# 64-bit weights converted in tiles of 512 columns, two in flight, instead of 256 columns, three in flight

## The chip, the core and the metric

The kernel runs on one core of a Trainium2 chip. The core has a matrix engine (TensorE, PE in the profile), an element-wise engine (VectorE, DVE), an activation engine (ScalarE, ACT), a general engine (GpSimd, POOL) and a queue from which this kernel issues all its DMAs (SyncE, SP). Each engine takes its own instructions in the order in which they were written into its queue, and waits at an instruction until what it needs is there. The metric is the device time of one execution, in microseconds (us).

## The reference, cut to what matters

Three stages follow each other on a batch of 8 sequences of 576 tokens and width 512.

1. Attention with 8 heads: a pack of 32 rows attends to the keys and values, and then the queries attend to the result. The output is `x`.
2. A channel mix: `xk` and `xr` are blends of `x` and of `x` one token earlier; `k = relu(xk @ w_k)`, `v = (k*k) @ w_v`, `r = sigmoid(xr @ w_r)`; the output is `r * v`.
3. A second mix: `u = x + (x^T U V)^T` along the tokens, then `u + relu(u @ w_ch1) @ w_ch2`.

The activations q, k, v, p come as 32-bit floats. The weights `w_k`, `w_v`, `w_r`, `U`, `V`, `w_ch1` and `w_ch2` come as **64-bit** floats, which no engine reads. So the kernel loads them as pairs of 32-bit words and rebuilds 32-bit floats from the bits: the high word holds sign, exponent and 20 bits of fraction, the low word the rest. That is the conversion which the change touches.

## The kernel before, in words

Matmuls with the weights run in three passes of a rounded format: each operand is split into a high part and a low remainder (`split`, line 868: one copy on ACT or DVE, one subtraction on DVE), and `PASS` multiplies high by high, high by low and low by high.

The batch is treated in 4 pairs of sequences. Attention is done in 16 units (4 for each pair). The first four units run interleaved at the start; the later ones run beside the channel mix of the pair before. The channel mix and the second mix go through 12 chunks of 384 tokens. For each chunk of the channel mix, `r_block` makes three outputs from `w_r`, `k_block(m)` eight from `w_k`, and `v_block(m)` adds eight contributions of `w_v`. The second mix comes after, chunk by chunk, and is made of matmuls that hold PE to the end.

**The order of the work** is not written by hand. Every operation is recorded in a `Plan`, and `emit` (line 333) makes a list schedule: at each step it takes the engine that can start first by its own cost table, and on this engine the ready operation with the lowest class (`cls`), and within a class the one that was ready first (PE and SP: the one recorded first). The result is a fixed order for each engine. Attention has class 0. The mixes have class 1. Conversions of `w_r` and of the first half of `w_k` have class 0, those of `w_v`, of the second half of `w_k` and of `U` class 1, those of `V`, `w_ch1` and `w_ch2` class 3.

**A conversion** (`Cast.run`, line 829) takes a tile of at most N = 256 columns. It loads it into `st`, 256 pairs of words, and then runs: ACT `a` = absolute value of the high words (line 853), DVE `h` = the high words, with values under a threshold set to nought (line 854), ACT `m` = the low words as a float, scaled (line 855), then DVE in turn: shift `h` into `a` (line 857), merge bits into `a` (858), keep sign and exponent in `h` (859), `m*h` (860), `m+a` (861), and last the split into the weight's two halves, or a store to DRAM. The high words lie 8 bytes apart in `st`; `h`, `a` and `m` are tiles of their own without gaps. There are 3 buffers of `st` and 3 of each of `h`, `a`, `m`. A buffer of `st` is free for the next load as soon as `a`, `h` and `m` have read it.

`cast_rows` (line 887) converts a weight tile of 128 rows by 512 columns in two such halves; a matmul waits for the column half that it reads. `w_r` is 4 tiles of 512 columns, `w_k` and `w_v` are 8 each, `w_ch1` and `w_ch2` 16 each. The loads of the first attention units are mixed with those of `w_r` (`FIRST`, line 502), and the loads that come after a `w_r` tile wait until that tile has its `st` buffer (`go`, line 902). The second half of `w_k` and `w_v` are converted in the order v0, v1, first column halves of `w_k`, v2, v3, second column halves of `w_k`, v4 to v7. From chunk 1 on, 9 conversions for the second mix are recorded in each chunk (`NPER`, line 1202); their results go to DRAM (`w1_d`, `w2_d`) and come back later.

Of the kernel before, what the change touches and what calls it, by code (L numbers as in the profile page):

```python
# [9 lines left out]
F32 = mybir.dt.float32  # L10
F32R = mybir.dt.float32r
I32 = mybir.dt.int32
# [457 lines left out]
def packed_attention_moe_mixer_kernel(  # L470
# [19 lines left out]
    NP = p.shape[2]  # L490
    P = 128
    DM = H * D
    NJ = DM // P
    NBP = B // 2
    NI = S // 64
    NC = NI // 3
    CW = 3 * P
    MK = w_k.shape[1] // P
# [9 lines left out]
    plan = Plan(nc)  # L508
    add, sub, mul = ALU.add, ALU.subtract, ALU.mult

    def open_pool(es, name, bufs, side):
        return es.enter_context(tc.tile_pool(name=name, bufs=bufs, side=side, reuse_waits="tile"))
# [8 lines left out]
    def dtile(name, shape, parts=(0,)):  # L521
        return plan.fixed(dram.tile(shape, F32, name=name), parts)
# [4 lines left out]
    v_d = dtile("v_d", [NP, S])  # L527
    w1_d = [dtile(f"w1_d{m}", [P, NJ * P]) for m in range(MC)]
    w2_d = [dtile(f"w2_d{m}", [P, DM]) for m in range(MC)]
# [289 lines left out]


    class Cast:
        N = 256

        def __init__(self, es, side):
            self.st = Pool(obj=open_pool(es, "cvst", 3, side), bufs=3)
            self.tp = Pool(obj=open_pool(es, "cvtp", 3, side), bufs=3)
            self.pools = [self.st, self.tp]

        def run(self, srcs, n, put=None, parts=None, after=()):
            N = self.N  # L830
            raw = srcs[0][1].dtype != F32
            st = plan.tile(self.st, [P, N * 2], I32, "st", parts=tuple(range(len(srcs))))
            for i, (rows, src) in enumerate(srcs):
                s = st.at(i)
                to = s[rows, 0:2 * n] if raw else s[rows, 0:n].bitcast(F32)
                if raw:
                    src = src.bitcast(I32)
                if src.shape[0] > P:
                    to = to.rearrange("p (a c) -> p a c", a=2)
                    src = src.rearrange("(a p) c -> p a c", p=P)  # L840
                plan.dma(to, src, after=after)
            if not raw:
                if parts is None:
                    put(st.bitcast(F32))
                else:
                    split(*parts, st.bitcast(F32)[:, 0:n])
                return st.alloc
            r = slice(srcs[0][0].start, srcs[-1][0].stop)
            sv = st.rearrange("p (n t) -> p n t", t=2)[r, 0:n]
            whole = [plan.tile(self.tp, [P, N], F32, tag) for tag in "ham"]  # L850
            h, a, m = [t[r, 0:n] for t in whole]
            top = sv[:, :, 1].bitcast(F32)
            plan.act(a, top, AF.Abs)
            plan.stt(h, a, 1.125 * 2.0 ** -15, top, ALU.is_ge, mul)
            plan.act(m, sv[:, :, 0].bitcast(U32), AF.Copy, scale=2.0 ** -52)
            hb, ab = h.bitcast(I32), a.bitcast(I32)
            plan.ts(ab, hb, 3, 0x3FFFFFF8, ALU.logical_shift_left, ALU.bitwise_and)
            plan.stt(ab, hb, -0x40000000, ab, ALU.bitwise_and, ALU.bitwise_or)
            plan.ts(hb, ab, -0x800000, None, ALU.bitwise_and)
            plan.tt(m, m, h, mul)  # L860
            plan.tt(m, m, a, add)
            if parts is None:
                put(whole[2])
            else:
                split(*parts, m)
            return st.alloc

    def split(hi, lo, src, engs=("dve",)):
        plan.copy(hi, src, ("act", "dve"))
        plan.tt(lo, src, hi, sub, engs)  # L870
# [6 lines left out]
    def wtile(pl, name):  # L877
        return plan.tile(pl, [P, 2, 512], F32R, name, parts=(0, 1))

    cast_cls = [0]  # L880
    cv = Cast(es_att, "right")
# [2 lines left out]
    A0 = Bufs(es_att, "A", "right", 8)  # L884
    AX_ = [A0] + [Bufs(es_st, n, "left", 4, True) for n in "BCD"]

    def cast_rows(t, src, halves=(0, 1)):
        for h in halves:
            plan.cls = cast_cls[0]
            to = [t.at(h)[:, i, h * 256:(h + 1) * 256] for i in range(2)]  # L890
            last = cv.run([(slice(0, P), src[:, h * 256:(h + 1) * 256])], 256, parts=to)
            plan.cls = 0
        return last

    wr = [wtile(w1a, f"wr{j}") for j in range(NJ)]
    wk = [[wtile(w1a, f"wk{j}_0")] for j in range(NJ)]
    plan.cls = 0
    go = ()
    for what in FIRST.split():
        u = int(what[1])  # L900
        if what[0] == "w":
            go = (cast_rows(wr[u], w_r[u * P:(u + 1) * P, :]),)
        elif what[0] == "p":
            load_p(u)
        else:
            {"k": AX_[u].load_k, "q": AX_[u].load_q, "v": AX_[u].load_v}[what[0]](u, go)
# [17 lines left out]
    for j in range(NJ):  # L924
        cast_rows(wk[j][0], w_k[j * P:(j + 1) * P, 0:512])
# [11 lines left out]
    wv = [wtile(w1b, f"wv{m}") for m in range(MK)]  # L937
# [3 lines left out]
    def cast_v(m):  # L941
        cast_rows(wv[m], w_v[m * P:(m + 1) * P, :])
# [1 line left out]
    cast_cls[0] = 1  # L944
    cast_v(0)
    cast_v(1)
    for h in range(2):
        for j in range(NJ):
            cast_rows(wk[j][1], w_k[j * P:(j + 1) * P, 512:1024], (h,))
        cast_v(2 + 2 * h)  # L950
        cast_v(3 + 2 * h)
    cast_v(6)
    cast_v(7)

    for b2 in range(2):
        r = slice(b2 * 64, (b2 + 1) * 64)
# [2 lines left out]
                  z.unsqueeze(1).to_broadcast([64, NI * 4, 32]), ("dve",))  # L959
    usv = ust.rearrange("p i (a b r) -> p i a b r", a=2, b=2)  # L960
    uv = U.rearrange("(p i) r -> p (i r)", i=NI)
    for i0, i1 in ((0, 5), (5, NI)):
        src = uv[:, i0 * NP:i1 * NP]

        def put_u(w, i0=i0, i1=i1):
            for b2 in range(2):
                r = slice(b2 * 64, (b2 + 1) * 64)
                s = w[r, 0:(i1 - i0) * NP].rearrange("p (i r) -> p i r", r=NP)
                split(usv[r, i0:i1, 0, b2, :], usv[r, i0:i1, 1, b2, :], s)

        cv.run([(slice(0, 64), src), (slice(64, P), src)], (i1 - i0) * NP, put_u)

    chunks = [(b, c) for b in range(NBP) for c in range(NC)]
    xin, xm, rt, kk_t, vps, ups = {}, {}, {}, {}, [], []
# [24 lines left out]
    def half(t, i):  # L999
        return t.at(i)[:, i, :]  # L1000

    def r_block(n, t):
        ps = plan.bank(ps_k, "psr")
        sl = slice(t * P, (t + 1) * P)
        i = 0
        for j in range(NJ):
            for a, w in PASS:
                plan.mm(ps, half(xm[n, 1, j], a)[:, sl], wr[j][:, w, :], start=(i == 0), stop=(i == 11))
                i += 1
        r = plan.tile(r_p, [P, 512], F32, "r")  # L1010
        rt[n, t] = r
        return plan.copy(r, ps)
# [5 lines left out]
    def k_block(n, m):  # L1018
        ps = plan.bank(ps_k, "psk")
        i = 0  # L1020
        sl = slice((m % 4) * P, (m % 4 + 1) * P)
        for j in range(NJ):
            for w, a in PASS:
                plan.mm(ps[:, 0:CW], wk[j][m // 4].at((m % 4) // 2)[:, w, sl], half(xm[n, 0, j], a),
                        start=(i == 0), stop=(i == 11))
                i += 1
        s = plan.tile(hid_p, [P, CW], F32, "s", name="sq")
        plan.act(s, ps[:, 0:CW], AF.Relu)
        plan.square(s, s)
        kk = plan.tile(kk_p, [P, 2, CW], F32R, "kk", parts=(0, 1))  # L1030
        split(half(kk, 0), half(kk, 1), s)
        kk_t[n, m] = kk

    def v_block(n, m):
        if m == 0:
            vps[:] = [plan.bank(ps_v, "psv") for _ in range(3)]
        kk = kk_t.pop((n, m))
        for t in range(3):
            for i, (a, w) in enumerate(PASS):
                plan.mm(vps[t], half(kk, a)[:, t * P:(t + 1) * P], wv[m][:, w, :],  # L1040
                        start=(m == 0 and i == 0), stop=(m == MK - 1 and i == 2))

    def x2_out(n, t):
# [150 lines left out]
        plan.dma(dst[:, 3 * c + t, :], o)  # L1194

    casts = []
    for c in range(3):
        def put_v(w, c=c):
            plan.dma(v_d[:, c * 192:(c + 1) * 192], w[0:NP, 0:192])
        casts.append((slice(0, NP), V[:, c * 192:(c + 1) * 192], 192, put_v))  # L1200
    NCAST = len(chunks) - 3
    CAST0, NPER = 1, 9
    for m in range(MC):
        for g in range(2):
            def put(w, m=m, g=g):
                plan.dma(w1_d[m][:, g * 256:(g + 1) * 256], w[:, 0:256])
            casts.append((slice(0, P), w_ch1[g * 256:(g + 1) * 256, m * P:(m + 1) * P], 256, put))
        for g in range(2):
            def put(w, m=m, g=g):
                plan.dma(w2_d[m][:, g * 256:(g + 1) * 256], w[:, 0:256])  # L1210
            casts.append((slice(0, P), w_ch2[m * P:(m + 1) * P, g * 256:(g + 1) * 256], 256, put))

    def finish(n):
        v_block(n, MK - 1)
# [6 lines left out]
    for n in range(len(chunks)):  # L1221
        b, c = chunks[n]
# [27 lines left out]
        if n >= CAST0:  # L1250
            plan.cls = 3
            for _ in range(len(casts) if n == NCAST else NPER):
                if casts:
                    rows, src, size, put = casts.pop(0)
# [16 lines left out]
    for n in range(len(chunks)):  # L1271
# [7 lines left out]
        for m in range(MC + 2):  # L1279
# [6 lines left out]
            if m >= 6 and prep:  # L1286
                kind, a = prep.pop(0)
# [42 lines left out]
```

## Time and profile before

| | us |
|---|---|
| median of 3 runs | 1618.4 (1616.36 to 1621.14) |
| the profiled execution, its own time | 1620.91 |
| its span in the trace | 1619.1 |
| PE busy | 1559.5 |
| DVE busy | 800.2 |
| ACT busy | 616.8 |

The span runs from the first instruction to the last; the execution's own time has 1.8 us more around it. Busy time is a share of the whole span, and the stages differ: DVE and ACT are busy while weights are converted and attention runs, in the first two fifths of the span, and nearly idle afterwards, when PE runs alone. PE's busy time counts matmuls at whichever clock was granted.

### The profile page before, as it was taken

To read this page: it belongs to the slowest core of one execution; us is meant where nothing else is said; L and a number is where in the kernel's file an instruction comes from. 1 tells how busy PE (TensorE), PEld (TensorE's weight loads), DVE (VectorE), ACT (ScalarE), POOL (GpSimd) and SP (SyncE) were. 2 spreads that over 40 slices of the span, in tenths; PEclk is the share of its full clock that TensorE was granted. 3 is DMA by queue.
4 is the path that set the end of the run, shared out by engine and by line. 5 is a ranking of instruction groups with operands and counts; after the bars stand their busy time and mean duration, and the time that the engine had idled before them with its cause. 6 is when DMAs were issued, how large, how long until landed. Compare 5 with 4: busy or idle time off the path is not lost.

```text
span 1619.1 us, 21662 instructions
## 1 busy us (share of the span) xinstructions
PE 1559.5 (96%) x8152; PEld 1384.9 (86%) x8152; DVE 800.2 (49%) x2035; ACT 616.8 (38%) x1442; POOL 3.0 (0%) x18
## 2 busy tenths in 40 slices
PE   7777889999999999999999999999999999999998
PEld 6566778888888888888889999999999989999997
DVE  5879887887888778764532222222222222221211
ACT  4767666666766666554321111111111111111110
POOL 0000000000000000000000000000000000000000
PEclk9889899999999999999999999999999999999999
DMA  9965445456453333330511101010010101101000
GB/s 184 214 165 140 124 123 137 136 137 168 132 134 122 128 93 112 109 108 20 167 61 46 46 1 39 1 46 13 27 39 1 40 1 40 40 0 40 0 20 20
DMA packets 156393, 128.57 MB, mean 79 GB/s; under 512 B 94145, under 2 KB 121473, under 8 KB 156289
## 3 DMA queue, kind: packets, MB, share of 16 engines
q1 hardware_dynamic: 156288, 127.19, 27.9%
q8 instruction: 64, 1.05, 0.3%
q14 instruction: 41, 0.33, 0.1%
HBM read 89.33 MB, written 37.82 MB: 79 GB/s over the span
## 4 chain that ended last, share of the span: by engine, by line
PE 91%; DVE 3%; ACT 2%; DMA 2%; SPq 1%; issue 1%; ACTq 0%; DVEq 0%
PE psc L197 49%; PE psv L197 12%; PE psk L197 12%; PE psr L197 6%; PE psat L197 6%; PE psat L208 2%; SPq L311 1%; PE psu L197 1%; PE psh L197 1%; PE pst L208 1%; ACT a L229 1%; DMA qin<-in_q_dram 1%; DMA s<-w_d 0%; DVE h L265 0%; DVE m L250 0%
## 5 line engine op out<-in xcount | busy, mean ns | idle before, releaser
L197 PE MATMUL psc<-ut,w 128*128 128x384 f32 x2304 | 433.9, 338 | 1.0 <-DVE hid L265 1.0
L197 PE MATMUL psc<-w,hid 128*128 128x512 f32 x1728 | 426.1, 393 | 1.1 <-ACT hid L229 1.1
L197 PEld LDWEIGHTS psc<-ut,w 128*128 128x128 f32 x2304 | 405.5, 188 | 13.1 <-DVE hid L265 1.4
L197 PEld LDWEIGHTS psc<-w,hid 128*128 128x128 f32 x1728 | 322.0, 188 | 60.9 <-ACT hid L229 1.5
L265 DVE SCALAR_TENSOR_TENSOR hid<-psc,hid 128x384 fp32r<-128x384 f32 x192 | 106.9, 557 | 466.1 <-ACT hid L229 466.0
L229 ACT ACTIVATE hid<-psc 128x384 fp32r<-128x384 f32 x192 | 94.2, 491 | 607.5 <-PE psc L197 607.5
L197 PE MATMUL psv<-wv,kk 128*128 128x512 f32 x864 | 227.9, 400 | 3.7 <-DVE wv L250 3.7
L197 PE MATMUL psk<-xk,wk 128*128 128x384 f32 x1152 | 227.7, 341 | 1.0 <-DVE xk L250 1.0
L197 PEld LDWEIGHTS psk<-xk,wk 128*128 128x128 f32 x1152 | 202.1, 189 | 7.6 <-DVE xk L250 1.5
L197 PEld LDWEIGHTS psv<-wv,kk 128*128 128x128 f32 x864 | 159.4, 189 | 32.9 <-DVE wv L250 4.3
L197 PE MATMUL psr<-wr,xr 128*128 128x512 f32 x432 | 111.0, 403 | 4.6 <-ACT xr L280 4.6
L197 PEld LDWEIGHTS psr<-wr,xr 128*128 128x128 f32 x432 | 81.6, 193 | 21.3 <-ACT xr L280 4.9
L250 DVE TENSOR_TENSOR kk<-sq,kk 128x384 fp32r<-128x384 f32 x96 | 52.6, 553 | 46.1 <-ACT kk L280 45.5
L229 ACT ACTIVATE sq<-psk 128x384 f32<-128x384 f32 x96 | 46.4, 486 | 69.4 <-PE psk L197 67.7
L229 ACT ACTIVATE m<-x,om_t 128x384 f32<-128x384 f32 x96 | 57.2, 610 | 12.3 <-DVE xk L250 6.0
L262 DVE SCALAR_TENSOR_TENSOR m<-x,mu_t,m 128x384 f32<-128x384 f32 x96 | 57.9, 611 | 3.8 <-ACT m L229 3.6
L250 DVE TENSOR_TENSOR ut<-pst,ut 128x512 fp32r<-128x512 f32 x36 | 24.9, 691 | 67.4 <-ACT ut L229 67.3
L229 ACT ACTIVATE a<-st 128x256 f32<-128x256 f32 (+2 forms) x109 | 45.8, 427 | 23.2 <-DVE m L250 16.5
L250 DVE TENSOR_TENSOR u<-psh,u 128x512 f32<-128x512 f32 x36 | 24.9, 691 | 51.0 <-PE psh L197 47.8
L229 ACT ACTIVATE m<-st 128x256 f32<-128x256 uint32 (+2 forms) x109 | 45.2, 426 | 7.1 <-DVE wv L250 2.7
L250 DVE TENSOR_TENSOR o<-psc,u 128x512 f32<-128x512 f32 x36 | 24.6, 688 | 46.5 <-PE psc L197 44.7
L229 ACT ACTIVATE ut<-pst 128x512 fp32r<-128x512 f32 x36 | 21.5, 598 | 67.6 <-PE pst L208 67.6
(134 smaller groups left out, 1527.3 us busy)
## 6 DMA issues: line engine op xcount, KB each, us to landing
st<-in_moe_w_ch_dram SPq DMA_DIRECT2D x64, 256.0 KB, 2.8
qin<-in_q_dram SPq DMA_DIRECT2D x32, 288.0 KB, 5.3
x_d<-xo SPq DMA_DIRECT2D x16, 576.0 KB, 3.4
x_d<-x SPq DMA_DIRECT2D x36, 256.0 KB, 3.7
u<-x_d SPq DMA_DIRECT2D x36, 256.0 KB, 3.4
out_dram<-o SPq DMA_DIRECT2D x36, 256.0 KB, 2.0
kin<-in_k_dram SPq DMA_DIRECT2D x32, 256.0 KB, 4.5
vin<-in_v_dram SPq DMA_DIRECT2D x32, 256.0 KB, 4.7
```

What stands on the lines that cost most here:

```text
L197: self.nc.tensor.matmul(o, l, r, start=start, stop=stop, **k)
L208: self.nc.tensor.transpose(out.get(), in_.get(), ident.get())
L229: self.nc.scalar.activation(o, in_.get(), func, **k)
L250: return self.elem(engs, lambda e, o, x, y: e.tensor_tensor(out=o, in0=x, in1=y, op=op), out, [a, b], self.TT, cls)
L262: ("dve",), lambda e, o, x, y, z: e.scalar_tensor_tensor(out=o, in0=x, scalar=z, in1=y, op0=op0, op1=op1), out, [a, b, s], {"dve": (1.042, ...
L265: ("dve",), lambda e, o, x, y: e.scalar_tensor_tensor(out=o, in0=x, scalar=s, in1=y, op0=op0, op1=op1), out, [a, b], self.TT, cls)
L311: self.nc.sync.dma_start(out=o, in_=i)
```

## The change

`N` becomes 512, with two buffers each instead of three. `h` is no tile any more: it is written over the high words in `st`, where they were loaded, so its elements lie 8 bytes apart. A weight tile is converted in one piece, and its matmuls wait for its high or its low part in whole. `w_k`'s second half is converted in one go, before v2. `U` goes in one piece instead of two, `V` in two instead of three, and 5 conversions are recorded in each chunk instead of 9.

```diff
     class Cast:
-        N = 256
+        N = 512
-            self.st = Pool(obj=open_pool(es, "cvst", 3, side), bufs=3)
-            self.tp = Pool(obj=open_pool(es, "cvtp", 3, side), bufs=3)
+            self.st = Pool(obj=open_pool(es, "cvst", 2, side), bufs=2)
+            self.tp = Pool(obj=open_pool(es, "cvtp", 2, side), bufs=2)
...
-            whole = [plan.tile(self.tp, [P, N], F32, tag) for tag in "ham"]
-            h, a, m = [t[r, 0:n] for t in whole]
-            top = sv[:, :, 1].bitcast(F32)
+            whole = [plan.tile(self.tp, [P, N], F32, tag) for tag in "am"]
+            a, m = [t[r, 0:n] for t in whole]
+            top = h = sv[:, :, 1].bitcast(F32)
             plan.act(a, top, AF.Abs)
             plan.stt(h, a, 1.125 * 2.0 ** -15, top, ALU.is_ge, mul)
             plan.act(m, sv[:, :, 0].bitcast(U32), AF.Copy, scale=2.0 ** -52)
-            hb, ab = h.bitcast(I32), a.bitcast(I32)
+            hb, ab = sv[:, :, 1], a.bitcast(I32)
...
-    def cast_rows(t, src, halves=(0, 1)):
-        for h in halves:
-            plan.cls = cast_cls[0]
-            to = [t.at(h)[:, i, h * 256:(h + 1) * 256] for i in range(2)]
-            last = cv.run([(slice(0, P), src[:, h * 256:(h + 1) * 256])], 256, parts=to)
-            plan.cls = 0
+    def cast_rows(t, src):
+        plan.cls = cast_cls[0]
+        last = cv.run([(slice(0, P), src)], 512, parts=[t.at(i)[:, i, :] for i in range(2)])
+        plan.cls = 0
...
-    for h in range(2):
-        for j in range(NJ):
-            cast_rows(wk[j][1], w_k[j * P:(j + 1) * P, 512:1024], (h,))
-        cast_v(2 + 2 * h)
-        cast_v(3 + 2 * h)
-    cast_v(6)
-    cast_v(7)
+    for j in range(NJ):
+        cast_rows(wk[j][1], w_k[j * P:(j + 1) * P, 512:1024])
+    for m in range(2, MK):
+        cast_v(m)
...
-    CAST0, NPER = 1, 9
+    CAST0, NPER = 1, 5
```

## Rows read from the trace of the kernel before

**Rows 1.** The page: busy time of each engine; then PE's and DVE's 40 slices.

```profile
PE 1559.5 (96%) x8152; PEld 1384.9 (86%) x8152; DVE 800.2 (49%) x2035; ACT 616.8 (38%) x1442; POOL 3.0 (0%) x18
...
PE   7777889999999999999999999999999999999998
...
DVE  5879887887888778764532222222222222221211
```

**Rows 2.** Windows: stretch, length, busy us per engine, PEclk, DMA share, GB/s.

```profile
38.00:95.70 57.70, 41.00 (x227) 32.44 (x226) 48.03 (x167) 38.99 (x121) 0.00 (x0) 0.86 0.87 216
95.70:216.00 120.30, 98.29 (x514) 80.29 (x515) 104.94 (x334) 82.68 (x222) 0.00 (x0) 0.91 0.55 141
...
240.00:675.00 435.00, 431.79 (x2370) 383.44 (x2370) 349.74 (x953) 281.64 (x661) 0.68 (x4) 1.00 0.45 130
```

**Rows 3.** Timeline, DVE then PE, 95 to 98 us: start, us, instruction, idle before.

```profile
94.99 0.41 DVE L250 TENSOR_TENSOR wk<-m,wk 128x256 fp32r<-128x256 f32 x1
95.32 0.16 DVE L256 TENSOR_SCALAR om_t<-mu_t 128x8 f32<-128x8 f32 x1
...
97.73 2.07 PE L197 MATMUL psr<-wr,xr 128*128 128x512 f32 x4 [4.64 <-ACT xr L280]
```

**Rows 4.** DVE's groups by shape: count, busy us, mean ns of one, idle before.

```profile
L265 DVE SCALAR_TENSOR_TENSOR h<-a,st 128x256 f32<-128x256 f32 x104 | 43.1, 417 | 5.1 <-ACT a L229 5.0
L265 DVE SCALAR_TENSOR_TENSOR a<-h,a 128x256 int32<-128x256 int32 x104 | 42.6, 417 | 0.1
...
L256 DVE TENSOR_SCALAR a<-h 128x256 int32<-128x256 int32 x104 | 28.9, 285 | 0.0
...
L283 DVE CAST w<-s 128x512 fp32r<-128x512 f32 x9 | 3.6, 424 | 3.0 <-DMA s<-w_d 3.0
...
L283 DVE COPY s_v<-raw_v 32x128 f32<-32x128 f32 x8 | 2.1, 268 | 0.0
...
L256 DVE TENSOR_SCALAR a<-h 128x128 int32<-128x128 int32 x1 | 0.2, 219 | 0.0
```

**Rows 5.** Timeline of DVE where it runs without a gap.

```profile
53.31 0.68 DVE L250 TENSOR_TENSOR a<-a,s 128x512 f32<-128x512 f32 x1
53.91 0.68 DVE L269 TENSOR_REDUCE s<-psat 128x16 f32<-128x512 f32 x1
...
79.97 0.29 DVE L256 TENSOR_SCALAR a<-h 128x256 int32<-128x256 int32 x1
80.17 0.42 DVE L250 TENSOR_TENSOR m<-m,a 128x256 f32<-128x256 f32 x1
80.50 0.29 DVE L256 TENSOR_SCALAR h<-a 128x256 int32<-128x256 int32 x1
```

**Rows 6.** Timeline of ACT: first `a` of four rounds of conversions, and one `m`.

```profile
121.15 1.09 ACT L229 ACTIVATE a<-st 128x256 f32<-128x256 f32 x3
...
136.33 0.46 ACT L229 ACTIVATE a<-st 128x256 f32<-128x256 f32 x1
...
141.81 0.42 ACT L229 ACTIVATE m<-st 128x256 f32<-128x256 uint32 x1
...
147.18 0.44 ACT L229 ACTIVATE a<-st 128x256 f32<-128x256 f32 x1
...
211.73 0.34 ACT L229 ACTIVATE a<-st 128x160 f32<-128x160 f32 x1
```

**Rows 7.** Timeline of DVE: the products `m*h` of the round that begins at 136.33.

```profile
145.32 1.08 DVE L250 TENSOR_TENSOR m<-m,h 128x256 f32<-128x256 f32 x3
```

**Rows 8.** SP's waits, 0 to 240 us (us in total, times, longest); landing of `w_v` loads.

```profile
SPq L311 <- ACT m L229: 43.6, 18, 11.5
...
st<-in_moe_w_v_dram SPq DMA_DIRECT2D x16, 256.0 KB, 3.3
```

More of the change, by code (lines that the diff above doesn't have):

```diff
@@ L838, in run @@
                 if src.shape[0] > P:
-                    to = to.rearrange("p (a c) -> p a c", a=2)
+                    to = to.rearrange("p (a c) -> p a c", a=src.shape[0] // P)
                     src = src.rearrange("(a p) c -> p a c", p=P)
@@ L862, in run @@
             if parts is None:
-                put(whole[2])
+                put(whole[1])
             else:
@@ L961, in packed_attention_moe_mixer_kernel @@
     uv = U.rearrange("(p i) r -> p (i r)", i=NI)
-    for i0, i1 in ((0, 5), (5, NI)):
+    for i0, i1 in ((0, NI),):
         src = uv[:, i0 * NP:i1 * NP]
@@ L1007, in r_block @@
             for a, w in PASS:
-                plan.mm(ps, half(xm[n, 1, j], a)[:, sl], wr[j][:, w, :], start=(i == 0), stop=(i == 11))
+                plan.mm(ps, half(xm[n, 1, j], a)[:, sl], half(wr[j], w), start=(i == 0), stop=(i == 11))
                 i += 1
@@ L1023, in k_block @@
             for w, a in PASS:
-                plan.mm(ps[:, 0:CW], wk[j][m // 4].at((m % 4) // 2)[:, w, sl], half(xm[n, 0, j], a),
+                plan.mm(ps[:, 0:CW], half(wk[j][m // 4], w)[:, sl], half(xm[n, 0, j], a),
                         start=(i == 0), stop=(i == 11))
@@ L1039, in v_block @@
             for i, (a, w) in enumerate(PASS):
-                plan.mm(vps[t], half(kk, a)[:, t * P:(t + 1) * P], wv[m][:, w, :],
+                plan.mm(vps[t], half(kk, a)[:, t * P:(t + 1) * P], half(wv[m], w),
                         start=(m == 0 and i == 0), stop=(m == MK - 1 and i == 2))
@@ L1196, in packed_attention_moe_mixer_kernel, with put1, put2 @@
     casts = []
-    for c in range(3):
+    for c in range(2):
         def put_v(w, c=c):
-            plan.dma(v_d[:, c * 192:(c + 1) * 192], w[0:NP, 0:192])
-        casts.append((slice(0, NP), V[:, c * 192:(c + 1) * 192], 192, put_v))
+            plan.dma(v_d[:, c * 288:(c + 1) * 288], w[0:NP, 0:288])
+        casts.append((slice(0, NP), V[:, c * 288:(c + 1) * 288], 288, put_v))
     NCAST = len(chunks) - 3
-    CAST0, NPER = 1, 9
+    CAST0, NPER = 1, 5
     for m in range(MC):
[L1204 to L1211, printed above, removed]
+        def put1(w, m=m):
+            plan.dma(w1_d[m], w)
+        casts.append((slice(0, P), w_ch1[:, m * P:(m + 1) * P], 512, put1))
+        def put2(w, m=m):
+            plan.dma(w2_d[m], w)
+        casts.append((slice(0, P), w_ch2[m * P:(m + 1) * P, :], 512, put2))
     def finish(n):
```

## The prediction, made before the changed kernel was run

> **What bounds the kernel now.** I read the page's slices first, then busy time by stretches, then the timelines of single engines where PE has gaps. PE is busy 96% of the span, but its slices show that the missing part lies at the front: from about the eighth slice on they read 9, before that 7 and 8, while DVE reads 7 to 9 there [rows 1]. The stretches say it in numbers [rows 2]: from 240 to 675 us PE idles 435.00 - 431.79 = 3.2 us, although the 67 conversions that are recorded behind `U` (3 of `V`, 64 for the second mix) run there; DVE has 85 us to spare. From 38 to 95.7 us PE idles 57.70 - 41.00 = 16.7 us, from 95.7 to 216 it idles 120.30 - 98.29 = 22.0 us, and DVE is busy 83% and 87% of them. So the change can be worth something only in the first 216 us, with the conversions of `w_r`, `w_k` and `w_v` (20 tiles of 512 columns, 40 halves now) and `U`. At most 39 us of PE's idle time are there to be won, less what attention needs anyway.
>
> Two places show how conversions set PE's pace. The first matmul of the channel mix starts at 97.73 us after a wait of 4.64 us for `xr` [rows 3]. The blend needs `om_t`, a tiny instruction of class 1, which DVE runs at 95.32, directly behind the last pieces of the first half of `w_k` (94.99): the class-0 conversions hold DVE until then. The second place is the stretch behind, where chunk 0 waits for `w_k`'s second half and `w_v`. Conversions run in rounds of three there, since three buffers are in flight. First `a` of a round starts at 121.15, 136.33, 147.18 and so on to 211.73, where `U` begins: 7 rounds in 90.6 us, 12.9 us each [rows 6].
>
> **DVE's work for a conversion.** In an unbroken run instructions start closer together than their durations: a product of 256 columns takes 0.42 us but the next starts after 0.33; a shift or mask takes 0.29 and the next starts after 0.20; one of 512 columns takes 0.68 and the next starts after 0.60 [rows 5]. So a half now holds DVE for 5 x 0.33 (lines 854, 858, 860, 861 and the subtraction of the split) + 2 x 0.20 (857, 859) = 2.05 us, and a tile of 512 for 4.1. After the change it is 5 x 0.60 for the five. A mask of 512 columns has no row, but a cast of 512 at the same rate lasts 424 ns [rows 4]; less the 0.08 us by which the next instruction overlaps, it holds DVE for 0.34. The sum is 5 x 0.60 + 2 x 0.34 = 3.68 us, 0.42 less for each tile.
>
> The high words are now read and written 8 bytes apart, where `h` was dense. For reading, the trace has the answer: line 854 reads them so today and takes 417 ns, as much as line 858 on dense tiles [rows 4]. For writing, and for the masks, which run at twice the rate (285 ns for 256 columns, not 417), no row has this step. From below, nothing: as with the read. From above, the nearest row is the copy `s_v<-raw_v`, whose source steps by 36 bytes: 268 ns for 128 columns against 219 for a dense mask of 128, so 49 ns for 128 columns [rows 4]. On the two masks and the one write of line 854 this makes 3 x 4 x 49 = 0.59 us for a tile, which eats the 0.42. I take nothing, because 8 bytes is nearest to the read of line 854, and keep both ends: 0.42 saved or 0.17 lost per tile.
>
> Here a rule of the Trainium skill speaks against the change. Its "Vector Engine (DVE) Microarchitecture Reference", section 5.2 (Measured stream behaviour on trn2), says that a port streams at full rate only while its elements come in pairs of adjacent words; elements that step one by one cost about 1.7 to 2.5 ns for a column instead of 1.05. By it line 854 ought to be slower today than line 858, and it is not, at a step of 8 bytes (417 and 417 ns, [rows 4]); this trace disagrees for reads and shows nothing for writes.
>
> **First stretch, to 95.7 us.** Eight tiles (`w_r`, first half of `w_k`) at 0.42 are 3.4 us less on DVE, in class 0, ahead of `om_t`. DVE idles 9.7 us of this stretch, and the last unit's `x` must be there too, so not all of it reaches the path: I take -2 us, with ends 0 and -3.4.
>
> **Second stretch, 95.7 to 216 us.** Now 24 halves make 8 rounds of 12.9 us, 103 us. After: 12 tiles, two in flight, 6 rounds of 1024 columns. A round gets more DVE work, 2 x 3.68 against 3 x 2.05, +1.2 us. It also loses prefetch. Now `st` is free when `m` has read it, at 141.81 + 0.42 = 142.2 in the round of 136.33 [rows 6], and the next round's data land while this one computes. After, `st` holds `h` and is free only behind `m*h`, at 145.32 + 1.08 = 146.4 [rows 7], 4.2 us later, and 0.8 us before the next round starts today (147.18). A load lands in 3.3 us at the median for half the bytes [rows 8], so up to 4 us of each round show; but two tiles need not run in step, and DVE has other work to fill in with. I take half, 2 us. A round then lasts 12.9 + 1.2 + 2 = 16.1 us, six of them 97 us: the last weight is ready 6 us earlier. If everything in this stretch moves up with it, that is the gain; if only the conversions move and PE merely fills its gaps sooner, it is 6 x 22.0 / 120.3 = 1.1 us. I take -4.
>
> ACT does `a`, `m` and often the copy of the split in one instruction instead of two. It is busy 69% of this stretch [rows 2], and its saving is taken as hidden behind DVE; without that cover it could add some 0.3 us a tile. A new order is that `m` reads a tile which DVE writes in line 854, so ACT's queue stands still if DVE is late there; behind it wait the softmax and the evictions of attention. I count this in the 2 us above. With the second half of `w_k` in whole ahead of v2, `k_block(4)` needs v0, v1 and 4 tiles, 3 rounds of 16.1 us, where it needed v0, v1 and 4 halves, 2.7 rounds of 12.9: 48 us against 34. But v2 and v3 then come right behind, and attention gives PE work in between. I cost it at nothing; without that cover, 14 us at PE's idle share would cost 14 x 22.0 / 120.3 = 2.6 us.
>
> **Later.** The 64 conversions for the second mix become 32, in a stretch where PE idles 3.2 us of 435: nothing. `V` and `NPER`: nothing, for the same reason.
>
> **The sum.** -2 - 4 = -6 us. The profiled execution took 1620.9 us, 2.5 above the median of the runs shown (1618.4); on the median, 1612.4, so I predict 1612. About 0.3%, 4.9 us, is what a measurement of this kernel can tell from no change, so this is hardly more than the least that would show.
>
> **Rivals.**
>
> (a) No change, about 1619: the written high words pay as the 36-byte copy does, 0.17 us lost a tile in place of 0.42 saved. The first stretch gets 8 x 0.17 = 1.4 us longer at most, and a round in the second lasts 16.1 + 2 x 0.59 = 17.3 us, which is 6 x 17.3 = 104 us against 103. For it: the masks move two elements at a time. Against it: line 854's read.
>
> (b) Slower, by late loads. If each load waits for the buffer that `m*h` frees, and nothing hides the 4.2 us, a round lasts 12.9 + 1.2 + 4.2 = 18.3 us. It decides from 8 x 12.9 / 6 = 17.2 us a round: above it, the conversions end later than today. At 18.3, six rounds last 110 us, +7, and the four rounds of the first stretch lose some 1 us in place of gaining 2, so about 1626. For it: SP already waits 43.6 us in 18 places for `m` to free `st` [rows 8], and loads of q, k and v stand behind in the same queue. Against it: 1024 columns in flight are a third more than 768.
>
> (c) Every step of 8 bytes pays. Five instructions of a tile then have an operand with this step that was dense (854, 857, 858, 859, 860): 5 x 4 x 49 = 0.98 us against 0.42 saved, 0.56 lost a tile. The first stretch gets 8 x 0.56 = 4.5 us longer, a round lasts 16.1 + 2 x 0.98 = 18.1 us, six 108: +5, so about 1628. Against it stands the read in line 854. The Trainium skill's "Vector Engine (DVE) Microarchitecture Reference", section 5.2, would have it go this way.
>
> (d) More, about 1603: two tiles out of step hide their loads wholly. A round lasts 14.1 us, six of them 85, 18 less; two thirds of that, as in the sum, move PE, and the first stretch gives 3.4: -15.
>
> **Chances.** Forecast 0.42, (a) 0.23, (b) 0.15, (c) 0.05, (d) 0.15. PE's clock spreads each of them: it was 0.86 and 0.91 of full speed in the two stretches [rows 2], so work that moves can gain or lose some 4 us. The forecast's own range is 1607 to 1617; (d) and (b) with that spread stretch it to 1601 and 1626, which leaves out about 2 in 10. Faster by over 0.3% (under 1613.5): two thirds of the forecast, (d), and 0.05 of (a), so 0.49. Within 0.3%: the rest of the forecast and most of (a), 0.30. Slower: (b), (c) and a little of (a), 0.21.
>
> **What would show it.** On DVE's groups by shape, masks of 512 columns near 420 ns and line 854 near 685 confirm the costs; masks well over 420, at 600 and more, confirm (a) or (c). `om_t` and the first matmul on `w_r` should start 2 us earlier. The first `a` of `U` should come near 203 us. SP's waits should name the product of line 860 as what frees `st`; if their total grows by over 20 us and first `a`s lie more than 17 us apart, (b) holds. PE's idle time from 675 us on must not change; if it does, the prediction is wrong in a place where I saw nothing.

## The result, and the profile after

The changed kernel takes 1604.85 us (1603.9 to 1605.97, 4 runs) against 1619.15 us (4 runs): a ratio of 0.9913, 95% interval 0.9896 to 0.993. It is 14.3 us faster. 6 us were forecast: the time lies below the forecast's own range (1607 to 1617) and inside the wider one (1601 to 1626), nearest to rival (d). As far as (d) goes that is luck, for its reason, rounds of 14.1 us, did not come about (16.5 below).

The profiled execution took 1604.63 us, with a span of 1602.8 us, 16.3 less than before. Page of the changed kernel: busy time, then the 40 slices of PE and DVE.

```profile
PE 1552.3 (97%) x8152; PEld 1379.0 (86%) x8152; DVE 776.7 (48%) x1687; ACT 605.6 (38%) x1316; POOL 3.1 (0%) x18
...
PE   7788899999999999999999999999999999999998
...
DVE  5889878778888777543632221222122222221211
```

PE's busy time fell by 1559.5 - 1552.3 = 7.2 us with the same 8152 matmuls, so they ran at a higher clock, and its idle time by (1619.1 - 1559.5) - (1602.8 - 1552.3) = 9.1 us [rows 1]. The idle time was saved in the first 240 us, 9.7 us there, and there the granted clock rose from 0.91 to 0.94; behind 240 us it is 1.00 in both kernels. Windows of the kernel before, then of the changed kernel, over the same stretches:

```profile
0.00:240.00 240.00, 191.36 (x1041) 156.30 (x1042) 195.26 (x636) 155.12 (x431) 1.32 (x11) 0.91 0.66 158
```

```profile
38.00:95.70 57.70, 43.75 (x249) 33.97 (x248) 49.45 (x133) 37.68 (x99) 0.00 (x0) 0.93 0.87 210
95.70:216.00 120.30, 105.55 (x552) 87.35 (x552) 105.56 (x250) 83.59 (x192) 0.00 (x0) 0.92 0.54 141
0.00:240.00 240.00, 201.03 (x1116) 165.05 (x1117) 195.36 (x511) 153.12 (x377) 1.47 (x11) 0.94 0.69 162
240.00:675.00 435.00, 431.44 (x2372) 383.41 (x2372) 343.06 (x773) 282.84 (x611) 1.64 (x7) 1.00 0.47 137
```

Read the two rows of 0 to 240 together. DVE is busy for the same time, 195.26 and 195.36 us, although each conversion costs it less: it got through more of its queue (the last part of `w_v` comes earlier, below), and PE, which needs what DVE makes, did 75 matmuls more at a granted clock of 0.94 instead of 0.91. PE's idle time fell from 48.6 to 39.0 us. That is how it looks when such an engine sets the pace. It is no proof: DVE also idles some 45 of the 240 us in both kernels. From 240 to 675 us PE idles 3.6 us instead of 3.2 [rows 2], and from 675 us to the end 7.2 instead of 7.6.

DVE's groups by shape in the changed kernel: the four instructions that read or write the high words with an 8-byte step in lines 854 to 859, and the dense sum of line 861 (`m<-m,a`) to compare them with (count | busy us, mean ns).

```profile
L265 DVE SCALAR_TENSOR_TENSOR st<-a,st 128x512 f32<-128x512 f32 x52 | 35.6, 687 | 5.5 <-ACT a L229 5.0
...
L265 DVE SCALAR_TENSOR_TENSOR a<-st,a 128x512 int32<-128x512 int32 x52 | 35.4, 684 | 0.2
L250 DVE TENSOR_TENSOR m<-m,a 128x512 f32<-128x512 f32 x52 | 35.4, 682 | 0.1
...
L256 DVE TENSOR_SCALAR st<-a 128x512 int32<-128x512 int32 x52 | 21.6, 421 | 0.1
L256 DVE TENSOR_SCALAR a<-st 128x512 int32<-128x512 int32 x52 | 21.5, 421 | 0.1
```

The step costs next to nothing, read or written: 687 ns where the write has it, 684 where only the read has it, 682 for the dense sum, and both masks keep their double rate at 421 ns, as a dense cast of 512 does (424, [rows 4]). So a tile holds DVE for about the 3.68 us that were worked out. That settles rivals (a) and (c) and the rule of the Trainium skill behind (c) ("Vector Engine (DVE) Microarchitecture Reference", section 5.2) for a step of 8 bytes: this trace disagrees with it, for reads and for writes.

Timeline of the changed kernel: `om_t` on DVE, the first matmul on `w_r`, and on DVE the last piece of the first half of `w_k`.

```profile
82.50 0.17 DVE L256 TENSOR_SCALAR om_t<-mu_t 128x8 f32<-128x8 f32 x1
...
86.53 2.55 PE L197 MATMUL psr<-wr,xr 128*128 128x512 f32 x10
...
98.04 0.69 DVE L250 TENSOR_TENSOR wk<-m,wk 128x512 fp32r<-128x512 f32 x1 [0.90 <-ACT wk L280]
```

The first two come 11 to 13 us earlier than before [rows 3], not 2. The last piece of the first half of `w_k` comes 3 us later (98.04 against 94.99): work of class 1 slipped in ahead of it. Timeline of ACT: first `a` of the round that begins with v0 (kernel before, then changed kernel), and in the changed kernel the start of the next round, of the last one and of `U`.

```profile
91.01 0.44 ACT L229 ACTIVATE a<-st 128x256 f32<-128x256 f32 x1 [1.28 <-DVE m L250]
```

```profile
91.01 0.67 ACT L229 ACTIVATE a<-st 128x512 f32<-128x512 f32 x1 [0.55 <-DMA st<-in_moe_w_v_dram]
...
114.25 0.71 ACT L229 ACTIVATE a<-st 128x512 f32<-128x512 f32 x1
...
180.38 0.66 ACT L229 ACTIVATE a<-st 128x512 f32<-128x512 f32 x1
...
196.86 0.46 ACT L229 ACTIVATE a<-st 128x288 f32<-128x288 f32 x1 [3.87 <-DMA st<-in_moe_U_dram]
```

The conversion of `w_v` starts at 91.01 us in both kernels. From 114.25 to 196.86 there are five rounds of 1024 columns, 16.5 us each; 16.1 was forecast. `U` starts at 196.86 instead of 211.73 [rows 6]. The last part of `w_v` moves further. DVE's subtractions that write `w_v`, in the kernel before and in the changed one (durations; first and last start, us):

```profile
L250 DVE TENSOR_TENSOR wv<-m,wv x16: 393/416/426, 120.3 to 215.6; 128x256 fp32r<-128x256 f32 x16
```

```profile
L250 DVE TENSOR_TENSOR wv<-m,wv x8: 666/684/693, 112.4 to 193.4; 128x512 fp32r<-128x512 f32 x8
```

It comes at 193.4 us instead of 215.6, 22.2 us earlier.

### The profile page after: what moved, and what is told of

Read it like the earlier page. It is cut to its first block, busy times and chain, and to the rows that moved or that the text cites. A ratio compares the mean times of both kernels' runs of the same rounds, so it can differ in the third digit from the quotient of the medians.

```text
span 1602.8 us, 20936 instructions
## 1 busy us (share of the span) xinstructions
PE 1552.3 (97%) x8152; PEld 1379.0 (86%) x8152; DVE 776.7 (48%) x1687; ACT 605.6 (38%) x1316; POOL 3.1 (0%) x18
## 4 chain that ended last, share of the span: by engine, by line
PE 91%; DVE 3%; SPq 2%; DMA 2%; ACT 2%; issue 1%; DVEq 0%; ACTq 0%
PE psc L197 49%; PE psv L197 12%; PE psk L197 12%; PE psr L197 6%; PE psat L197 5%; PE psat L208 3%; SPq L311 2%; PE psh L197 1%; PE psu L197 1%; PE pst L208 1%; DMA st<-in_moe_w_k_dram 1%; ACT a L229 0%; DMA qin<-in_q_dram 0%; DVE m L250 0%; DMA s<-w_d 0%
## 5 line engine op out<-in xcount | busy, mean ns | idle before, releaser
L197 PE MATMUL psk<-xk,wk 128*128 128x384 f32 x1152 | 234.7, 344 | 3.5 <-ACT xk L280 1.6
L229 ACT ACTIVATE a<-st 128x512 f32<-128x512 f32 (+2 forms) x55 | 35.6, 656 | 21.1 <-DMA st<-in_moe_w_ch_dram 5.2
L280 ACT ACTIVATE kk<-sq 128x384 fp32r<-128x384 f32 x76 | 39.5, 522 | 7.7 <-PE psv L197 5.1
```

The costliest lines, as they stand in the source:

```text
L197: self.nc.tensor.matmul(o, l, r, start=start, stop=stop, **k)
L229: self.nc.scalar.activation(o, in_.get(), func, **k)
L280: self.nc.scalar.activation(o, i, AF.Copy)
```

## Experiments

Two theories. **A**: the gain comes from what is in flight (1024 columns instead of 768) and from gaps between the class-0 conversions, into which class 1 slips. **B**: DVE sets the pace in the first 200 us, and the gain is its saved time. Each kernel was run beside the kernel before; ratios have their 95% interval in brackets.

**DVE's time given back (e1).**

```diff
             plan.ts(hb, ab, -0x800000, None, ALU.bitwise_and)
+            plan.ts(hb, hb, -0x800000, None, ALU.bitwise_and)
```

> The changed kernel with the mask of line 859 done twice in place: 0.34 us more on DVE for a tile, which gives back four fifths of the 0.42 us that the wider tile saves there. Theory A (more columns in flight, 1024 against 768, and gaps that let class 1 in; DVE's time is secondary): 1604 to 1608 us. Theory B (DVE's saved time sets the pace): most of the gain is lost, 1613 to 1618 us.

1612.64 us, ratio 0.9954 [0.9942, 0.9967]: half of the gain is gone. By the ratios this is 0.0041 x 1619 = 6.6 us above the changed kernel for 20 x 0.34 = 6.8 us of DVE work. The time lies 0.4 us below the range of B and 4.6 above that of A, so it speaks for B. Its first 240 us: DVE as busy as ever, PE 8 us less busy than in the changed kernel.

```profile
0.00:240.00 240.00, 193.05 (x1036) 157.01 (x1037) 195.70 (x509) 149.34 (x373) 1.33 (x11) 0.90 0.65 158
```

**Columns in flight with narrow tiles (e2), and writing in place alone (e3).** Kernel before, `h` over the loaded words, N = 256:

```diff
-            self.st = Pool(obj=open_pool(es, "cvst", 3, side), bufs=3)
+            self.st = Pool(obj=open_pool(es, "cvst", 4, side), bufs=4)   # e2 only, tp likewise
...
-            top = sv[:, :, 1].bitcast(F32)
+            top = h = sv[:, :, 1].bitcast(F32)
...
-            hb, ab = h.bitcast(I32), a.bitcast(I32)
+            hb, ab = sv[:, :, 1], a.bitcast(I32)
...
```

> The kernel before with h written in place and four buffers of 256 columns: 1024 columns in flight and the same memory as the changed kernel, but twice the instructions. Theory A (columns in flight): most of the gain, 1605 to 1611 us. Theory B (fewer and wider DVE instructions): none of it, 1617 to 1622 us.

> The kernel before with h written in place and nothing else: three buffers of 256 columns, each held until the product of line 860. Theory A: buffers come free later with no more of them, so a little slower than before, 1619 to 1627 us. Theory B: DVE has the same work, 1617 to 1621 us.

e2: 1625.08 us, 1.0025 [1.0017, 1.0034]. e3: 1617.39 us, 0.9976 [0.9964, 0.9987]. The same memory and the same 1024 columns in flight as the changed kernel give no gain but a small loss, so A falls in its first half. Writing in place gains a little by itself, and with a fourth buffer it loses a little, which takes e2 above the range of B too. Both runs have DVE's old work, and by the ratios they lie 4 us to either side of the kernel before. So something other than DVE's work moves the time by some 4 us; whether that is the order of the work, the buffers or their later release is not told apart here.

**`om_t` early (e4).**

```diff
-    plan.ts(om_t, mu_t, -1.0, 1.0, mul, add)
+    plan.ts(om_t, mu_t, -1.0, 1.0, mul, add, cls=0)
```

> The kernel before with the one small instruction that writes om_t in class 0 instead of class 1, so that the first blend does not wait for the class-0 conversions. If the late om_t alone held the first matmul on w_r at 97.7 us: that matmul starts some 5 to 10 us earlier and the kernel takes 1608 to 1614 us. If the blends of class 1 behind it are held just as long by the conversions: 1617 to 1621 us and the first such matmul at 95 us or later.

1621.26 us, 1.0005 [0.9993, 1.0016]. Timeline of PE in e4:

```profile
68.80 1.20 PE L197 MATMUL psr<-wr,xr 128*128 128x512 f32 x4 [1.25 <-ACT xr L280]
```

The first matmul on `w_r` starts at 68.8 us, 29 earlier, and the kernel gains nothing: a miss for both branches, since the cause was right and the effect was not. From 38 to 95.7 us PE does 241 matmuls instead of 227, and from 95.7 to 130 us 148 instead of 157: it filled an earlier gap and waited later. So `om_t` alone, slipping into such a gap, is not the gain; that was the second half of A, as far as it was tried.

**DVE's time taken away (e5), and given back late only (e6).** e5 drops line 859; the low word's part of the weights is then wrong. e6 repeats the mask only in the conversions for the second mix:

```diff
-            plan.ts(hb, ab, -0x800000, None, ALU.bitwise_and)   # e5
...
+            for _ in range(0 if plan.cls < 3 else 1):           # e6
+                plan.ts(hb, hb, -0x800000, None, ALU.bitwise_and)
```

> The changed kernel without the mask of line 859 (its output is then not the reference's): 0.34 us less on DVE for each tile, the counterpart of the run that does the mask twice. Theory B (DVE's time in the first 200 us sets the pace, about one for one): 20 tiles give 7 us, so 1596 to 1600 us. Theory A (columns in flight and gaps; DVE's time is secondary): 1602 to 1606 us. If the run with the mask done twice was slower only because the list schedule came out otherwise, this one can fall on either side.

> The changed kernel with the mask done twice in the conversions for the second mix alone (V, w_ch1, w_ch2; 34 of the 55), where PE idles 3.6 us in 435. Theory B says that DVE's time counts only before about 200 us: 1603 to 1607 us. If instead the later conversions carry a part of the gain: 1609 to 1615 us.

e5: 1595.78 us, 0.9844 [0.9831, 0.9858], by the ratios 11 us under the changed kernel for 6.8 us of DVE work. e6: 1604.69 us, 0.9901 [0.9888, 0.9915], no difference. DVE's time counts early and not late, as B has it.

**ACT's time (e7) and the loads (e9).**

```diff
             plan.act(m, sv[:, :, 0].bitcast(U32), AF.Copy, scale=2.0 ** -52)
+            plan.act(m, sv[:, :, 0].bitcast(U32), AF.Copy, scale=2.0 ** -52)   # e7
...
...
-                plan.dma(to, src, after=after)                                 # e9, weight tiles
+                for g in range(2):
+                    c = slice(g * n, (g + 1) * n)
+                    plan.dma(st.at(g)[rows, c], src[:, c], after=after)
```

> The changed kernel with ACT's m computed twice, 0.54 us more on ACT for each tile, more than the 0.37 us that the wider tile saves there. If DVE alone sets the pace: 1603 to 1608 us. If ACT's shorter work carries the part of the gain that DVE's does not explain (some 6 us): 1610 to 1618 us.

> The changed kernel where each 128x512 weight tile of w_r, w_k and w_v is loaded by two DMAs of 256 columns, as many DMAs and as short rows as before the change, and converted in one piece. If fewer and longer loads carry the part of the gain that DVE's time does not explain (some 3 to 5 us): 1607 to 1611 us. If DVE's time is all: 1603 to 1606 us.

e7: 1605.17 us, 0.9908 [0.9892, 0.9923]; e9: 1606.86 us, 0.9924 [0.9912, 0.9937]. ACT's time is hidden. e9 falls between its two ranges: the loads may be worth 1 or 2 us, but the intervals of e9 and of the changed kernel overlap, so that is not shown.

**One buffer (e10).**

```diff
-            self.st = Pool(obj=open_pool(es, "cvst", 2, side), bufs=2)
+            self.st = Pool(obj=open_pool(es, "cvst", 1, side), bufs=1)   # tp likewise
```

> The changed kernel with one buffer instead of two: 512 columns in flight, DVE's work the same. If DVE's work sets the pace whatever is in flight: under 1612 us. If a round's latency does (a round of two tiles takes 16.5 us; one tile alone some 5.5 us of engine work, 4 us of loading and the waits between): 20 tiles at 10 to 14 us end at 220 to 290 us instead of 194, so 1615 to 1650 us.

1679.04 us, 1.0369 [1.0355, 1.0383], worse than expected. The first matmul on `w_r` starts at 60.15 us here, the earliest of all, but the last part of `w_v` comes at 252 us. The last conversion for the second mix is stored at 795 us instead of 676, and PE waits behind 800 us too, 875.00 - 840.73 = 34 us, 27.3 of them in one wait for the second mix's first `X`; that the late conversions hold up this `X` is likely, but was not traced. Window of e10:

```profile
800.00:1675.00 875.00, 840.73 (x4248) 758.19 (x4248) 213.08 (x366) 136.47 (x262) 0.76 (x2) 0.98 0.11 35
```

So DVE's time sets the pace only while a second tile covers the wait of the first.

**DVE's work moved to GpSimd (e8).**

```diff
-            plan.tt(m, m, h, mul)
-            plan.tt(m, m, a, add)
+            plan.tt(m, m, h, mul, ("dve", "pool"))
+            plan.tt(m, m, a, add, ("dve", "pool"))
```

> The changed kernel where the list schedule may put the products and sums of lines 860 and 861 on GpSimd, which is idle. Theory B: up to 1.2 us less on DVE for each tile, so faster if GpSimd's own time, by the cost table twice DVE's, does not lengthen the rounds: 1588 to 1600 us. Theory A: each buffer is held longer, with no more of them: 1605 to 1615 us.

1612.78 us, 0.9953 [0.994, 0.9965]: some 7 us slower than the changed kernel, in the range of A and outside that of B. The timelines of DVE and of GpSimd in e8 show something that the expectation had left out (start, us):

```profile
83.10 0.55 DVE L250 TENSOR_TENSOR xr<-m,xr 128x384 fp32r<-128x384 f32 x1
83.57 1.63 DVE L262 SCALAR_TENSOR_TENSOR m<-x,mu_t,m 128x384 f32<-128x384 f32 x1
85.13 1.77 DVE L265 SCALAR_TENSOR_TENSOR st<-a,st 128x512 f32<-128x512 f32 x1
...
87.55 0.41 DVE L256 TENSOR_SCALAR a<-st 128x512 int32<-128x512 int32 x1
```

```profile
83.31 1.48 POOL L250 TENSOR_TENSOR m<-m,st 128x512 f32<-128x512 f32 x1 [3.76 <-ACT m L229]
84.87 1.48 POOL L250 TENSOR_TENSOR m<-m,a 128x512 f32<-128x512 f32 x1
```

A DVE instruction of 0.61 us lasts 1.63 when a GpSimd product began before it, and ends 0.4 us after that product; the next one, 0.69 us elsewhere, lasts 1.77 and ends 0.55 us after the second. 80 products and sums went to GpSimd, and yet DVE's busy time over the whole span grew, from 776.7 to 791.6 us.

That this is what made the kernel slower is not shown. The last part of `w_v` comes at 194.4 us, only 1 us later than in the changed kernel, and over the whole span PE idles 51.9 us against 50.5. Most of the loss lies in PE's own busy time, 1558.2 us against 1552.3 for the same matmuls, with a granted clock of 0.91 against 0.94 in the first 240 us. What lowered the clock there stays open.

**The same DVE work without the wide tile (e12).** Kernel before, 256 columns, three in flight, `h` apart; line 859 dropped as in e5.

> The kernel before (256 columns, three in flight, h apart) without the mask of line 859 (the low word's part is then computed wrong): 2 x 0.20 = 0.40 us less on DVE for each 512 columns, as much as the change saves there, and nothing else changed. Theory B (DVE's time is the whole gain): 1604 to 1608 us. If the wider tile gives something besides, in ACT, loads, waits or the order of the work: 1609 to 1614 us. If DVE's time is not what counts: 1616 to 1621 us.

1600.68 us, 0.9872 [0.9856, 0.9888]. With 0.40 us less DVE work per 512 columns and no other edit, the kernel before gains 20 us, more than the change did; the two intervals don't overlap. The time lies below all three ranges that were given: DVE's time counts, and for more than B had it.

**A version that follows from B (e11).** The changed kernel, the low word's three top bits put straight into the fraction:

```diff
-            plan.act(m, sv[:, :, 0].bitcast(U32), AF.Copy, scale=2.0 ** -52)
...
-            plan.ts(hb, ab, -0x800000, None, ALU.bitwise_and)
-            plan.tt(m, m, h, mul)
-            plan.tt(m, m, a, add)
+            plan.stt(ab, sv[:, :, 0], 29, ab, ALU.logical_shift_right, ALU.bitwise_or)
...
```

> A version that follows from theory B: the changed kernel where the low word adds its top three bits to the fraction by one shift-and-or on DVE (the float is cut instead of rounded, by less than one unit of the last place); ACT's m, the mask, the product and the sum of lines 855 and 859 to 861 go. DVE holds 4 x 0.60 + 0.34 = 2.74 us for a tile instead of 3.68, 0.94 less. Theory B, 20 tiles, one for one or somewhat more: 1580 to 1588 us. If the waits of attention now set the pace: 1590 to 1600 us.

1590.91 us, 0.9825 [0.9812, 0.9839]: 28 us faster than the kernel before, 14 faster than the changed one, the fastest of all here. B had put it at 1580 to 1588; it came out in the range given for the case that attention's waits set the pace. Window of e11: here DVE's busy time falls, to 188 of 240 us, and PE idles 31.6 us, its longest waits being those of attention.

```profile
0.00:240.00 240.00, 208.44 (x1179) 172.70 (x1180) 187.95 (x484) 150.03 (x378) 1.32 (x11) 0.96 0.69 168
```

## Why the prediction came out as it did

Right: where the change counts (the first 216 us, nothing later: e6); DVE's cost of a tile, 3.68 us against 4.10; no charge for the 8-byte step; a round of 16.1 us (16.5 measured); ACT hidden (e7); what frees `st`. SP's waits of the changed kernel, 0 to 240 us, name DVE's `m`, in total 7 us more than ACT's `m` did [rows 8], far from the 20 that would have meant rival (b):

```profile
SPq L311 <- DVE m L250: 50.7, 10, 17.6
```

Mis-sized, by more than a factor of two: the term of the second stretch, -4. Two things went into it. Its "now" was 8 rounds of 12.9 us, 103 us, but only seven rounds had been measured. The first, from 91.01 to 121.15, lasts 30 us, with attention and the first blends on DVE in between; from v0's first `a` to that of `U` it was 121 us. It became 106, so `U` moved up by 14.9 us instead of 6. Nearly all of the error is in that first round: it shrank from 30.1 to 23.2 us, where the sum let it grow from 12.9 to 16.1. The other rounds went from 90.6 us for seven to 82.6 for five, 8 us less where the sum had 10. And I took two thirds of the move as gain, between "all of it" and "PE only fills its gaps". The span gained 16.3 us, somewhat more than `U` moved and three quarters of the 22.2 us by which the last part of `w_v` moved; so the fraction was not far off, and the size of the move was.

Wrong: the first stretch, -2. The conversions did not get ahead there at all: `w_v` starts at 91.01 us in both kernels, and the first half of `w_k` ends 3 us later. PE did get ahead, with 249 matmuls from 38 to 95.7 us instead of 227, but with 241 there e4 gained nothing. I let `om_t` behind the class-0 conversions stand for the path. `om_t` moved by 12.8 us, and e4 moved it and the first matmul further, for nothing. An instruction that waits behind a busy engine shows that the engine is busy; that the kernel waits for this instruction does not follow. One slip of addition besides: the chance of "faster" comes to 0.28 + 0.15 + 0.05 = 0.48, not 0.49.

What the runs show of the cause: DVE's time for the 20 early tiles counts (B). With 512 columns the ratio goes 0.9825, 0.9844, 0.9913, 0.9954 for 2.74, 3.34, 3.68, 4.02 us of DVE work a tile (e11, e5, changed kernel, e1). Between the last three that is 1.6 and 1.0 us of the kernel's time for 1 us of DVE's (11.2 and 6.6 us for 6.8 each); from e5 to e11 it is a quarter (3 us for 12). The 4 us of e2 and e3 stand beside each of these steps, so one for one is as good a reading as any of the first two. The change saves 20 x 0.42 = 8.4 us of DVE's work, and 14.3 were gained. In the profiled executions PE's idle time fell by 9.1 us, and the other 7.2 us are matmuls that ran at a higher clock. The prediction had the clock only as spread, in both directions. In most runs a higher clock goes with fewer gaps: over the first 240 us, runs in which PE idles 31 to 41 us were granted 0.93 to 0.96 in the mean, those with 46 to 58 us 0.88 to 0.91. But e8, with 40 us, was granted 0.91, so it is not shown that the gaps decide it.

Open: e12 gained 20 us where DVE's 8 us would give 8 to 13. Dropping or doubling line 859 (e1, e5, e12), and e11, change not only how long DVE is held but also how long one tile's chain from load to weight lasts. No run changes one for the early tiles and leaves the other as it was, so whether DVE's total work or the length of that chain sets the pace is argued, not shown; that DVE idles some 45 of the first 240 us leaves room for the chain. Some 4 us, moreover, move without any of DVE's work (e2, e3). Whether the wide tile with two in flight costs something besides what it saves on DVE can't be told from these. The wide tile with `h` apart, or three of them in flight, was not tried.

## What to carry to other kernels

Before pricing a wait, ask whether the engine behind it stays equally busy when its work gets cheaper: then count its work, instruction by instruction at the spacing of starts, and take about all of it, not a share of PE's idle time, as the middle of the forecast. Here a step gave back from a quarter (e5 to e11) to two and a half times of it (e12). Measure the span from the first round to the last, not the mean of the regular ones. And take work off the busy engine by removing it (e11); giving it to an engine that holds the busy one up gained nothing (e8).

## What the runs showed of the hardware that was not expected

A product on GpSimd holds up DVE. In e8 a product or sum of 512 columns takes 1.42 to 1.49 us on GpSimd in the mean, and DVE instructions that begin during one end some 0.4 to 0.55 us after it. Groups of DVE in e8, first 216 us, then the same group of the changed kernel:

```profile
L262 DVE SCALAR_TENSOR_TENSOR m<-x,mu_t,m 128x384 f32<-128x384 f32 x18 | 15.1, 844 | 0.0
L256 DVE TENSOR_SCALAR a<-st 128x512 int32<-128x512 int32 x20 | 11.7, 591 | 0.1
```

```profile
L262 DVE SCALAR_TENSOR_TENSOR m<-x,mu_t,m 128x384 f32<-128x384 f32 x18 | 10.7, 609 | 0.0
...
L256 DVE TENSOR_SCALAR a<-st 128x512 int32<-128x512 int32 x20 | 8.3, 420 | 0.0
```

The mean rises from 609 to 844 ns for an instruction with two tensor inputs and from 420 to 591 for one of the two masks. The Trainium skill states this in "SBUF — State Buffer", section "Who interferes with whom": DVE instructions with two inputs in SBUF, or in a mode that uses both ports, share a port pair with GpSimd, and whichever starts first holds it for its whole instruction. The timeline of e8 agrees, with 0.61 us grown to 1.63; the same instruction, begun at 89.76 us, 0.2 us ahead of a product, kept its 0.60. Whether DVE holds up GpSimd in the same way was not looked at.

A write or read of 32-bit words 8 bytes apart costs DVE next to nothing at 128x512 (684 to 687 ns against 682 dense), and nothing in the double-rate masks: 421 ns against 424 for a dense cast.
